# DeltaNet and mixture of depths: 16x16 block inverses on VectorE, joined on TensorE, without the way over DRAM

## The chip, the cores and the metric

One NeuronCore of a Trainium2 chip runs the program. The metric is the device time of one execution in microseconds (us). A profiled execution has a span, from its first to its last instruction, and a time of its own, a little longer.

## The reference

The program has two parts. The first is a delta-rule recurrence over 768 tokens for 4 batches and 8 heads, with 48 values per head:

```python
for t in range(S):
    kt, vt, bt = (k_n[:, :, t], v[:, :, t], beta[:, :, t, None])
    y[:, :, t] = np.einsum('bhd,bhde->bhe', q[:, :, t], state)
    v_old = np.einsum('bhde,bhd->bhe', state, kt)
    state = state + bt[:, :, :, None] * np.einsum('bhd,bhe->bhde', kt, vt - v_old)
```

Here `k_n` is k divided by its norm. The second part takes y as x (768 tokens of 384 values per batch), scores every token with `w_gate`, chooses 128 tokens of each batch, and gives those `x + sigmoid(score) * relu(x @ w1) @ w2`. All other tokens pass through. All arithmetic is in float32.

## The kernel before, in words

**Chunks.** The recurrence runs over chunks of 64 tokens. A chunk works on 2 batches and 8 heads at once, 16 (batch, head) pairs; there are 24 chunks, 12 for each half of the batches. Inside a chunk the recurrence is a triangular system of 64 unknowns. Its matrix comes from the products of all keys of the chunk with each other (`products`, tile `g`). It is solved by inverting the two 32x32 triangles on its diagonal, and then using them and the 32x32 block below: `z` (L667) makes M from the lower block and the lower inverse, and the recurrence makes W = T V and adds M W1.

**Elimination.** Four chunks are inverted together (`eliminate(e)`, L513, six of them): 4 partition groups of 32 (batch and half) hold 32 triangles each, and VectorE works on all 128 partitions with up to 32x32 values in each. To bring one triangle into one partition's row, the first elimination uses a VectorE transpose (L523). The others write `g` to DRAM (`spill`, L464) and read it back turned, into tile `a` (L528). After scaling (L563), 27 steps follow, each with a product (`mul`, L586, into `tmp`), a row (L572) and an addition (`add`, L592); the last six rows are done one by one. A product with a table of factors ends it (L597). The first and last elimination turn their result back with VectorE (L600), the last then copies it to tile `tt` by DMA; the four others write it to DRAM (`ad`, L604) and read it back turned into `tt` (L610).

**Recurrence.** Chunk i (`recur`, L711) is a chain between TensorE and ScalarE: `mm_r` (L734, keys times state), copy to `v` (L741), `mm_w` (L749 with `tt`, or L755 in four 32-row parts with `g`), copy W1 to `wsb` (L771), `mm_m` (L766), two copies to `wbd` (L775), `mm_s` (L783, the new state in `psta`), copy to `s` (L788). Beside it `mm_q` (L797) and `mm_p` (L809) make the output, `out_x` copies it (L815), and VectorE scores it (L829). Transposes of k and q (L395), their products (L454) and the ranking of tokens (`ranking`, L881) are put in between. The dense part (`depths`, L977, with L1025 and L1041) comes mostly after the last chunk.

**Order.** A planner in the kernel (`Plan`, L25) decides the order of every engine's operations when the program is built. Each operation has an engine, a duration, operations it depends on, a latency to its users, a priority, and buffers that it takes and gives back. The planner plays this through in time and writes out the order in which operations start. Where it sees TensorE idle, it puts in matmuls of ones as fillers (L301). Its durations do not wait for anything on the chip; they only set the order. All instructions are written out one after the other, without loops on the chip. PSUM has one tile for the state and a ring of three pairs of banks (`pair`) for all else.

Of the kernel before, what the change touches and what calls it, by code (L numbers as in the profile page):

```python
# [15 lines left out]
P = 128  # L16
# [141 lines left out]
def kernel(  # L158
# [30 lines left out]
    assert NB == HC and NCH % BC == 0 and H == 8  # L189
    DP = 64  # L190
# [36 lines left out]
    ring("a", 2, [HC, HC])  # L227
    rings["gd"] = [dram.tile([P, NB, C], FP32, name=f"gd{m}") for m in range(3)]
    plan.ring("gd", 3)
    ad = [dram.tile([P, HC, HC], FP32, name=f"ad{m}") for m in range(2)]  # L230
    ring("mb", 1, [HC, HC])
    ring("zt", 3, [GP, HC])
    ring("tt", 2, [NB, C])
# [19 lines left out]
    def maker(eng, own=0.0, lat=0.15):  # L253
# [9 lines left out]
        ("PE", 0.0, 0.22), ("ACT", 0.0, 0.12), ("DVE", 0.12, 0.2), ("POOL",), ("SP",))]  # L263
# [25 lines left out]
    wsb = sbuf("wsb", [GP, D])  # L289
# [21 lines left out]
    ds = [slice(x * DP, x * DP + D) for x in range(2)]  # L311
    four = [(0, 0), (1, 1), (0, 1), (1, 0)]
# [4 lines left out]
    def constants():  # L317
# [6 lines left out]
        for t in rings["tt"]:  # L324
            nc.gpsimd.memset(t, 0.0)
# [87 lines left out]
    def prep(i):  # L413
# [72 lines left out]
        for nm in "kq":  # L486
# [4 lines left out]
            n["t" + nm] = pe(0.48, emit, n["l" + nm] + late, v, take=[kx, (nm + "t", i)],  # L491
                             give=[("q", i)] if nm == "q" else [], work=512,
                             lat=0.22 if first else LATE["turn"], **h)
            if first and nm == "k":
                n["ek"] = [on(0.38, put(par, eng), [n["tk"]], v, give=[kx], **h)
                           for par, on, eng in ((0, act, nc.scalar), (1, dve, nc.vector))]
            else:
                n["e" + nm] = [act(0.6, both, [n["t" + nm]], v, give=[kx], **h)]
        gt = [kb] + [("g", e)] * (i % BC == 0)
        if first:  # L500
            n["g"] = pe(1.0, first_products, n["ek"], u, take=gt, work=1024, hard=True)
            n["eg"] = [act(0.59, out_g, [n["g"]], u, give=[kb], hard=True)]
        else:
            n["g"] = pe(0.75, products("kt", kb), [*n["ek"], N[e * BC].get("g")], u, take=gt,
                        work=1024, lat=LATE["g"])
            n["eg"] = [act(0.6, out_g, [n["g"]], u, give=[kb])]
            n["sg"] = sp(0.6, spill, n["eg"], u, take=[("gd", e)] * (i % BC == 0), lat=4.6)
        v = 10 * i - 14
        n["w"] = pe(0.75, products("qt", kw), n["eq"] + n["ek"] + [N.get(("end", 0))], v,
                    work=1024, take=[kw, ("p", i)], lat=LATE["p"])  # L510
        n["ep"] = [dve(0.7, out_p, [n["w"]], v - 200, give=[kw])]

    def eliminate(e):  # L513
        u = 40 * e - 50
        s = N["e", e] = {}
        first = e == 0

        over = 0 < e < NE - 1
        hard = dict(hard=first)

        def turn_in():
            if first:
                nc.vector.transpose(out=got("a", e),  # L523
                                    in_=got("g", e)[:, :, HC:].rearrange("p n t -> p t n"))
                return
            for par in range(2):
                for hf, rows in ((0, lo[par]), (1, hi[par])):
                    nc.sync.dma_start(  # L528
                        out=got("a", e)[rows],
# [3 lines left out]
        def diag():  # L533
            nc.vector.tensor_scalar_max(
                nrm[:, 0], got("a", e).rearrange("p i c -> p (i c)")[:, ::HC + 1], 1e-30)
# [15 lines left out]

        def table():

            b, sign = bh[e % 2], -1 if over else 1
            nc.gpsimd.affine_select(  # L555
                out=got("mb", e), pattern=[[sign, HC], [-sign, HC]], base=0,
                in_=(b[:, :, None] if over else b[:, None, :]).to_broadcast([P, HC, HC]),
                channel_multiplier=0, compare_op=ALU.is_ge, fill=0.0)

        def scale():  # L560
            a = got("a", e)
            b = bh[e % 2]
            nc.vector.tensor_tensor(out=a, in0=a, op=ALU.mult,  # L563
                                    in1=(b[:, None, :] if over else b[:, :, None])
                                    .to_broadcast([P, HC, HC]))
            nc.vector.memset(a.rearrange("p i c -> p (i c)")[:, ::HC + 1], 1.0)

        def row(i, j):
            a = got("a", e)
            to, of = (a[:, :j, i], a[:, :j, j]) if over else (a[:, i, :j], a[:, j, :j])  # L570
            by = a[:, j, i:i + 1] if over else a[:, i, j:j + 1]
            nc.vector.scalar_tensor_tensor(out=to, in0=of, scalar=by, in1=to,  # L572
                                           op0=ALU.mult, op1=ALU.add)

        def step(j):
            w = HC - 2 - j

            def view():
                return tmp[j % 2][:, :w * j].rearrange("p (i c) -> p i c", c=w if over else j)

            def mul():
                a = got("a", e)
                x = ((a[:, j:j + 1, j + 2:], a[:, :j, j:j + 1]) if over else
                     (a[:, j + 2:, j:j + 1], a[:, j:j + 1, :j]))
                shape = [P, j, w] if over else [P, w, j]
                nc.vector.tensor_tensor(out=view(), op=ALU.mult, in0=x[0].to_broadcast(shape),  # L586
                                        in1=x[1].to_broadcast(shape))

            def add():
                a = got("a", e)  # L590
                to = a[:, :j, j + 2:] if over else a[:, j + 2:, :j]
                nc.vector.tensor_tensor(out=to, in0=to, in1=view(), op=ALU.add)  # L592
            return mul, add, 0.075 + 1.04e-3 * w * j

        def final():
            a = got("a", e)
            nc.vector.tensor_tensor(out=a, in0=a, in1=got("mb", e), op=ALU.mult)  # L597

        def turn_out():
            nc.vector.transpose(out=got("g", e)[:, :, HC:].rearrange("p n t -> p t n"),  # L600
                                in_=got("a", e))

        def out_a():
            nc.sync.dma_start(out=ad[e % 2], in_=got("a", e))  # L604


        def back(par):
            def emit():
                for hf, rows in ((0, lo[par]), (1, hi[par])):
                    nc.sync.dma_start(out=got("tt", e)[rows, :, hf * HC:(hf + 1) * HC],  # L610
                                  in_=ad[e % 2][rows].rearrange("n i c -> i n c") if over else
                                  got("g", e)[rows, :, HC:])
            return emit
# [10 lines left out]
        N["nrm", e] = s["nt"] = dve(0.2, turn_n, [s["sc"]], u + 2)  # L624
        s["mb"] = pool(1.6, table, [s["sc"]], u, take=[("mb", e)])
        last = dve(1.45, scale, [s["sc"]], u, **hard)

        nxt, rest = last, [last]
        for j in range(1, HC - 1):
            if j >= HC - 4:  # L630
                rows = [dve(0.16, (lambda i=i, j=j: row(i, j)), [nxt, *rest], u, **hard)
                        for i in range(j + 1, HC)]
                nxt, rest = rows[0], rows
                continue
            mul, add, dur = step(j)
            m = dve(dur, mul, [nxt], u, **hard)
            nxt = dve(0.13 + 1.04e-3 * j, (lambda j=j: row(j + 1, j)), [nxt, *rest], u, **hard)
            rest = [dve(dur, add, [m, *rest], u, **hard)]
            if j == HC - 8:
                N["late", e] = rest[0]  # L640
        N["end", e] = last = dve(1.22, final, [nxt, *rest, s["mb"]], u, give=[("mb", e)], **hard)
        if over:
            x = plan.add("DVE", 0.0, lambda: None, [last], u, lat=1.5)
            s["to"] = sp(0.69, out_a, [x], u, take=[("tt", e)], give=[("a", e)], lat=4.0)
# [492 lines left out]
```

## Time and profile before

| | |
|---|---|
| median of 4 runs | 344.81 us (340.48 to 348.99) |
| the profiled execution's own time | 338.85 us |
| its span | 337.1 us |
| granted TensorE clock, mean | 0.852 |
| instructions | 17,651 |
| TensorE matmuls, weight loads | 7866, 7866 |
| DMA | 37.60 MB, mean 112 GB/s |

In the lines of the profile, PE is TensorE's matmuls, PEld its weight loads, DVE VectorE, ACT ScalarE, POOL GpSimd, SP the engine that issues most DMAs. `out<-in` names tiles, `128x64` is partitions by elements, `64*64` the rows and columns of TensorE's array that an instruction uses, `x32` a number of instructions. A float32 matmul of the kernel is two matmul instructions with a weight load each; transposes and bfloat16 ones are one. In the chain of waits, each piece of the span is put down to the instruction, DMA or queue that the end of the program waited for; "issue" is time in which an engine waited for nothing that the profile shows. In the list of DMA queues, the columns are packets, MB and the share of 16 engines' time; the kind "instruction" brings the engines' code. A row of the windows has the stretch, its length, then busy time (and number of instructions) of PE, PEld, DVE, ACT and POOL, then the granted clock, the DMA engines' busy share and GB/s.

### The profile page before, as it was taken

To read this page: it belongs to the slowest core of one execution; us is meant where nothing else is said; L and a number is where in the kernel's file an instruction comes from. 1 tells how busy PE (TensorE), PEld (TensorE's weight loads), DVE (VectorE), ACT (ScalarE), POOL (GpSimd) and SP (SyncE) were. 2 spreads that over 40 slices of the span, in tenths; PEclk is the share of its full clock that TensorE was granted. 3 is DMA by queue.
4 is the path that set the end of the run, shared out by engine and by line. 5 is a ranking of instruction groups with operands and counts; after the bars stand their busy time and mean duration, and the time that the engine had idled before them with its cause. 6 is when DMAs were issued, how large, how long until landed. Compare 5 with 4: busy or idle time off the path is not lost.

```text
span 337.1 us, 17651 instructions
## 1 busy us (share of the span) xinstructions
PE 280.9 (83%) x7866; PEld 221.9 (66%) x7866; DVE 217.8 (65%) x856; ACT 131.6 (39%) x299; POOL 26.8 (8%) x51
## 2 busy tenths in 40 slices
PE   7498496997959876976977979989988999999994
PEld 4446445776737765864866868878777788576571
DVE  4169999499993999679585499798455423522000
ACT  2219203554513545342552554443646344112110
POOL 8120002001000100010000010000020000031011
PEclk9769878799876978795696795696988799999999
DMA  6796687362688667576987756343631021110000
GB/s 95 133 159 137 152 216 130 70 162 46 160 204 187 147 167 164 117 150 145 200 219 192 141 107 124 72 94 64 126 75 51 4 47 31 26 49 25 25 23 23
DMA packets 127691, 37.60 MB, mean 112 GB/s; under 512 B 119552, under 2 KB 123776, under 8 KB 127616
## 3 DMA queue, kind: packets, MB, share of 16 engines
q1 hardware_dynamic: 120048, 33.65, 46.7%
q10 hardware_dynamic: 7056, 1.26, 2.3%
q0 software_dynamic: 512, 1.57, 1.5%
q8 instruction: 61, 1.00, 1.3%
q14 instruction: 14, 0.11, 0.1%
HBM read 23.10 MB, written 12.85 MB: 107 GB/s over the span
## 4 chain that ended last, share of the span: by engine, by line
PE 48%; DMA 16%; DVE 16%; issue 8%; SPq 6%; ACT 5%; POOLq 0%; ACTq 0%; DVEq 0%
PE pair L1025 5%; DMA ad<-a 5%; PE psta L783 5%; PE pair L1041 5%; PE pair L809 5%; PE pair L766 4%; DVE tmp L586 4%; DMA tt<-ad 4%; PE pair L301 4%; DVE a L592 4%; PE pair L797 3%; PE psta L734 3%; SPq L610 3%; PE pair L749 3%; PE pair L454 3%
## 5 line engine op out<-in xcount | busy, mean ns | idle before, releaser
L586 DVE TENSOR_TENSOR tmp<-a 128x29 f32<-128x29 f32 (+8 forms) x162 | 54.4, 336 | 0.0
L592 DVE TENSOR_TENSOR a<-a,tmp 128x29 f32<-128x29 f32 (+8 forms) x162 | 53.1, 328 | 0.0
L572 DVE SCALAR_TENSOR_TENSOR a<-a 128x28 f32<-128x28 f32 (+29 forms) x198 | 46.0, 240 | 0.1
L704 DVE TENSOR_TENSOR psta<-v,nnT 128x192 f32<-128x192 f32 x44 | 16.0, 365 | 27.1 <-ACT v L741 26.4
L783 PE MATMUL psta<-wbd,k 128*64 128x96 f32 x352 | 27.3, 307 | 4.7 <-ACT wbd L775 4.5
L775 ACT COPY wbd<-pair 64x384 f32<-64x384 f32 x48 | 22.7, 473 | 19.2 <-PE pair L766 17.8
L809 PE MATMUL pair<-wbd,p 128*64 128x96 f32 x384 | 27.8, 303 | 0.0
L766 PE MATMUL pair<-wsb,zt 32*32 32x48 f32 x768 | 23.0, 212 | 5.7 <-ACT wsb L771 4.8
L301 PE MATMUL pair<-warm 128*128 128x512 bf16 x84 | 27.6, 470 | 0.0
L783 PEld LDWEIGHTS psta<-wbd,k 128*64 128x64 f32 x352 | 21.4, 174 | 8.8 <-ACT wbd L775 7.5
L766 PEld LDWEIGHTS pair<-wsb,zt 32*32 32x32 f32 x768 | 19.4, 112 | 10.0 <-ACT wsb L771 8.7
L1025 PE MATMUL pair<-xeT,w_sb 128*64 128x128 f32 x384 | 23.5, 275 | 2.2 <-ACT hT L1032 2.2
L555 POOL TENSOR_SCALAR_AFFINE_SELECT mb<-bh 128x1024 f32<-128x1024 f32 x6 | 10.5, 1752 | 175.3 <-DVE bh L547 114.3
L809 PEld LDWEIGHTS pair<-wbd,p 128*64 128x64 f32 x384 | 22.8, 176 | 1.6
L1025 PEld LDWEIGHTS pair<-xeT,w_sb 128*64 128x64 f32 x384 | 20.9, 137 | 4.0 <-ACT hT L1032 2.9
L917 DVE TENSOR_SCALAR_CACHE_REDUCE mk<-rep 128x64 bf16<-128x64 f32 (+10 forms) x22 | 13.3, 607 | 15.7 <-ACT rep L910 15.6
L1041 PE MATMUL pair<-w_sb,hT 128*64 128x384 f32 x128 | 22.3, 490 | 0.0
L797 PE MATMUL pair<-s,qt 64*64 64x48 f32 x704 | 20.1, 262 | 2.2 <-issue 2.2
L771 ACT COPY wsb<-pair 128x384 f32<-128x384 f32 x24 | 11.5, 479 | 24.7 <-PE pair L749 21.3
L797 PEld LDWEIGHTS pair<-s,qt 64*64 64x64 f32 x704 | 17.0, 174 | 5.7 <-issue 4.3
L741 ACT COPY v<-psta 128x384 f32<-128x384 f32 x22 | 10.6, 480 | 23.8 <-PE psta L734 22.5
L460 ACT COPY g<-pair 128x512 f32<-128x512 f32 x24 | 14.0, 593 | 13.8 <-PE pair L444 7.5
(113 smaller groups left out, 454.8 us busy)
## 6 DMA issues: line engine op xcount, KB each, us to landing
gd<-g SPq DMA_DIRECT2D x20, 256.0 KB
q<-in_q_dram SPq DMA_DIRECT2D x48, 96.0 KB
v<-in_v_dram SPq DMA_DIRECT2D x48, 96.0 KB
out_dram<-x SPq DMA_DIRECT2D x20, 192.0 KB
k<-in_k_dram SPq DMA_DIRECT2D x36, 96.0 KB
a<-gd SPq DMA_DIRECT2D x20, 128.0 KB
ad<-a SPq DMA_DIRECT2D x4, 512.0 KB
tt<-ad SPq DMA_DIRECT2D x16, 128.0 KB
```

Source lines behind the costliest of these rows:

```text
L301: nc.tensor.matmul(rings[name][k][:, 0], lhsT=warm[:, :P], rhs=warm, start=True, stop=True)
L572: nc.vector.scalar_tensor_tensor(out=to, in0=of, scalar=by, in1=to, op0=ALU.mult, op1=ALU.add)
L586: nc.vector.tensor_tensor(out=view(), op=ALU.mult, in0=x[0].to_broadcast(shape), in1=x[1].to_broadcast(shape))
L592: nc.vector.tensor_tensor(out=to, in0=to, in1=view(), op=ALU.add)
L704: nc.vector.tensor_tensor(out=to[:, b], in0=x, in1=y, op=ALU.mult)
L766: nc.tensor.matmul(pw[hi[par], bb, y], lhsT=zt[lo[par], bb * GI + y], rhs=wsb[lo[par], bb * GI + y], start=False, stop=True, skip_group_ch ...
L775: nc.scalar.copy(wb[half[par], :, par].rearrange("p (b r) d -> p b r d", b=2), heads(kw)[half[par]])
L783: nc.tensor.matmul(psta[half[a % 2], r // 2, r % 2 * 2 * D:(r % 2 + 1) * 2 * D], lhsT=t[:, a], rhs=wb[:, a].rearrange("p h d -> p (h d)"), ...
L797: nc.tensor.matmul(py[half[bb], rt, x * D:(x + 1) * D], lhsT=qt[half[rt], bb * 2 + h4, half[par]], rhs=s_old[half[rt], bb * 2 + h4, par], ...
L809: nc.tensor.matmul(py[half[bb], rt, h4 * 2 * D:(h4 + 1) * 2 * D], lhsT=t[:, a], rhs=wb[:, a].rearrange("p h d -> p (h d)"), start=(c == 0 ...
L1025: nc.tensor.matmul(ps[half[x]], lhsT=w1_sb[:, t, c0:c0 + C], rhs=got("xeT", b)[:, t], start=(t == 0), stop=(t == KD - 1))
L1041: nc.tensor.matmul(got("pair", b, "o")[c0:c1, 0, :DM], lhsT=got("hT", b)[:, f, c0:c1], rhs=w2_sb[:, f], start=(f == 0), stop=(f == KF - 1))
```

## The change

Each 32x32 triangle is taken as two 16x16 triangles and the block below. VectorE inverts the 64 small triangles of each partition, two at a time in each instruction: 14 steps of a product and an addition, each dependent on the one before. The single rows are gone. Two VectorE transposes then bring the result into tiles `ta` and `tb`, in all eliminations alike; `ad`, `tt` and their DMAs are gone. The way from `g` over DRAM into `a` stays.

For each chunk TensorE joins the halves: `up_z` is 32 products of 32x32 with 16 columns (64 instructions), ScalarE copies them to `zs`, `up_t` puts the transposed triangle in PSUM through the identity (4 products) and adds 32 more products, 72 instructions in all, and ScalarE copies the result back to `ta`. `z` then uses `ta`. `mm_w` has the 32 products of the L755 form for all chunks. `mm_m` uses four 32x32 tiles of TensorE's array where it used two, so M lies on all 128 partitions (`zt` at half the width), and W1 is copied there in three pieces. GpSimd makes the factor table in two 16x16 parts. The planner's durations are set anew. In the built order TensorE has 11,690 matmuls; 36 fillers remain of 84.

```diff
+    QC = HC // 2
-    ad = [dram.tile([P, HC, HC], FP32, name=f"ad{m}") for m in range(2)]
-    ring("zt", 3, [GP, HC])
-    ring("tt", 2, [NB, C])
+    ring("zs", 2, [GP, QC])
+    ring("zt", 3, [GI, HC])
+    ring("ta", 2, [NB, HC])
+    ring("tb", 2, [NB, HC])
...
         def step(j):
-            w = HC - 2 - j
+            w = QC - 1 - j
...
+            def mul():
+                a, shape = blocks("a"), [P, 2, w, j]
+                nc.vector.tensor_tensor(
+                    out=view(), in0=a[:, :, j + 1:, j:j + 1].to_broadcast(shape),
+                    in1=a[:, :, j:j + 1, :j].to_broadcast(shape), op=ALU.mult)
+
+            def add():
+                a = blocks("a")[:, :, j + 1:, :j]
+                nc.vector.tensor_tensor(out=a, in0=a, in1=view(), op=ALU.add)
...
+        def turn_a():
+            nc.vector.transpose(out=got("ta", e).rearrange("p n t -> p t n"), in_=whole("a"))
+
+        def turn_b():
+            nc.vector.transpose(out=got("tb", e).rearrange("p n t -> p t n"),
+                                in_=whole("a").rearrange("p i c -> p c i"))
...
+        four_rows = [(rows[bb], hf) for bb in range(GB) for hf, rows in ((0, lo), (1, hi))]
...
+        def up_z():
+            g, t, ps = got("g", e), got("ta", e), bank(0)
+            for x in range(GP):
+                for rows, hf in four_rows:
+                    c0 = HC if e == 0 else hf * HC
+                    nc.tensor.matmul(ps[rows, x], lhsT=g[rows, n0 + x, c0:c0 + HC],
+                                     rhs=t[rows, n0 + x, QC:], start=True, stop=True)
+
+        def out_z():
+            nc.scalar.copy(got("zs", i), bank(0))
+
+        def up_t():
+            ta, tb, z, ps = got("ta", e), got("tb", e), got("zs", i), bank(1)
+            for rows, _ in four_rows:
+                nc.tensor.matmul(ps[rows], lhsT=ident[rows, rows], rhs=ta[rows, n0:n0 + GP, QC:],
+                                 start=True, stop=False, skip_group_check=True)
+            for x in range(GP):
+                for rows, _ in four_rows:
+                    nc.tensor.matmul(ps[rows.start:rows.start + QC, x],
+                                     lhsT=tb[rows, n0 + x, :QC], rhs=z[rows, x],
+                                     start=False, stop=True, skip_group_check=True)
+
+        def out_t():
+            nc.scalar.copy(got("ta", e)[:, n0:n0 + GP, QC:], bank(1))
...
         def mm_w():
-                    if not n["direct"]:
-                        nc.tensor.matmul(pw[half[par], bb, y],
-                                         lhsT=got("tt", e)[half[bb], ch * GP + a],
-                                         rhs=x[half[bb], a], start=(y == 0), stop=False,
-                                         skip_group_check=True)
-                        continue
                     for rows in (lo, hi):
-                        nc.tensor.matmul(pw[rows[par], bb, y],
-                                         lhsT=got("g", e)[rows[bb], ch * GP + a, HC:],
+                        nc.tensor.matmul(pw[rows[par], bb, y], lhsT=t[rows[bb], ch * GP + a],
...
         def mm_m():
-                for bb in range(GB):
-                    for par in range(2):
-                        nc.tensor.matmul(pw[hi[par], bb, y], lhsT=zt[lo[par], bb * GI + y],
-                                         rhs=wsb[lo[par], bb * GI + y], start=False,
-                                         stop=True, skip_group_check=True)
+                for bb, par in four:
+                    rows = at[bb][par]
+                    nc.tensor.matmul(pw[hi[par], bb, y], lhsT=zt[rows, y], rhs=w1[rows, y],
+                                     start=False, stop=True, skip_group_check=True)
...
         def out_w1():
-            nc.scalar.copy(wsb.rearrange("p (b r) d -> p b r d", b=2), heads(kw))
+            pw = heads(kw)
+            nc.scalar.copy(w1[:3 * HC], pw[:3 * HC, 0])
+            for par in range(2):
+                nc.scalar.copy(w1[hi[par]], pw[lo[par], 1])
```

## The prediction

> **What bounds the kernel now.** I read the page first, then the chain of waits, then TensorE's timeline, then the DMA packets. The page (parts 1, 3 and 4):
>
> ```profile
> PE 280.9 (83%) x7866; PEld 221.9 (66%) x7866; DVE 217.8 (65%) x856; ACT 131.6 (39%) x299; POOL 26.8 (8%) x51
> q8 instruction: 61, 1.00, 1.3%
> PE 48%; DMA 16%; DVE 16%; issue 8%; SPq 6%; ACT 5%; POOLq 0%; ACTq 0%; DVEq 0%
> ```
>
> No engine is full. The chain is PE for half, and DMA, DVE and SPq for 38%. Where DVE and DMA stand on it, the chain from 82 to 100 us shows the way from the end of an elimination to the first product that uses it:
>
> ```profile
> 87.65 0.10 DVE a L592
> 87.75 4.19 DMA ad<-a
> 92.37 1.53 SPq L610
> 94.55 2.77 DMA tt<-ad
> 97.36 0.99 PE pair L673 x62
> ```
>
> 9.6 us pass between 87.75 and 97.36. The same stretch takes 11.6 us from 119.01, 8.9 from 151.63 and 9.3 from 187.86: 39.4 us in all. This is what the change goes for. But 8% of the chain, some 26 us, is "issue": PE waits for nothing that is computed. TensorE's timeline around 53 and 171 us shows where:
>
> ```profile
> 51.80 1.17 PE L673 MATMUL pair<-g 32*32 32x32 f32 x96
> 52.83 0.76 PE L755 MATMUL pair<-v,g 32*32 32x48 f32 x60
> 55.87 0.27 PE L755 MATMUL pair<-v,g 32*32 32x48 f32 x4 [2.29 <-issue]
> ...
> 169.85 0.50 PE L797 MATMUL pair<-s,qt 64*64 64x48 f32 x20
> 171.36 0.43 PE L797 MATMUL pair<-s,qt 64*64 64x48 f32 x12 [1.01 <-issue]
> ```
>
> PE stops in the middle of one operation, 60 instructions into 64, whose operands have long been there. Queue q8 tells why. It brought 1.00 MB in 61 packets, 16 KB each; PE's program has 15,820 instructions (7866 matmuls, 7866 weight loads, 88 others), so a packet holds 256 of them, 128 pairs of load and matmul. I listed the packets' times and numbered PE's instructions in program order. If packet n brings the instructions from number 464 + 256n on, no packet's first matmul starts earlier than 1.34 us after the packet has ended, in any of the 61, and 17 start within 1.8 us: there PE was waiting for its own code. The packet at 53.51 to 54.43 is the one that PE resumes with at 55.87. Nor is a packet begun early: where PE stood at such a border, the next one began 0.8 to 2.8 us after it went on. So the code comes in a loop with one packet under way: start, 0.9 to 1.5 us of packet, 1.4 us until PE goes on, then the next. Five borders at which PE waited follow one at which it had waited too; from one to the next took 3.82, 4.33, 4.04 us (around 172 us, DMA share 0.82) and 3.98, 3.73 us (240 to 248 us, share near 0.45). Never in the trace do two packets start less than 3.46 us apart. The rate of matmuls agrees (windows of 10 us):
>
> ```profile
> 255.00:265.00 10.00, 8.64 (x316) 7.51 (x310) 4.80 (x23) 6.22 (x15) 0.00 (x0) 0.83 0.17 43
> 265.00:275.00 10.00, 8.66 (x343) 7.58 (x341) 4.74 (x17) 4.47 (x10) 0.00 (x0) 1.00 0.01 3
> 275.00:285.00 10.00, 10.00 (x307) 8.73 (x299) 3.13 (x14) 4.79 (x12) 0.00 (x0) 1.00 0.27 64
> ```
>
> 31 to 34 matmuls per us is 128 in 3.7 to 4.2 us: in its densest stretches the kernel already runs close to the pace of that loop.
>
> **The change part by part.**
>
> *Elimination on VectorE.* Out go 27 steps of three instructions and six single rows. In come 14 steps of two, on 2wj elements (w = 15 - j), 1120 in one pass. Rows of L586 go from 199 ns at 56 elements to 388 at 225: 137 ns + 1.1 ns each. So 28 x 0.137 + 2 x 1.23 = 6.3 us, and 0.04 between dependent ones (L542 to L547 show it): 7.3. The first elimination scales from 22.88 us on (L563 halved, 0.7; small ones 0.2), runs its steps (7.3), lets the same v products through (1.2), multiplies by the table (L597, 1.2) and transposes once (1.95): ready at 35.4 us, where now the first z product starts at 51.8. The second transpose (1.95) lies beside TensorE's first products.
>
> *No turn over DRAM.* The 39.4 us above go, with 24 DMA issues of SP (0.3 to 1.7 us each in the L610 rows). Late next on this path would be up_z, ACT, up_t, ACT, z: about 4 us at full clock.
>
> *TensorE, time.* Per chunk up_z adds 64 instructions and up_t 72. The nearest row is z, 32x32 in four tiles: 32 start within 263 ns, 383 until the next operation (168.15). So 0.65 and, with the four copies by the identity, 0.85. The W product has 64 instructions everywhere (0.73, L755 at 63.95) instead of 32 (0.50 to 0.61): +0.2 in 19 chunks. M W1 in four tiles instead of two goes from 0.80 (L766) to about 0.4. Together +1.3 us a chunk, 31 us in all, of which idle PE and 48 dropped fillers can take most.
>
> *TensorE, code.* 136 pairs x 24 + 32 x 19 - 48 fillers = 3824 pairs more: 11,690 instead of 7866, and 23,456 instructions, 91.6 packets instead of 61.8. In the built order the first up_z stands at packet 4.4 and the last product of the recurrence at 85.8: 81.4 packets. Now the same stretch (4.4 to 56.05, 35.7 to 288.6 us) has 51.6, at 4.9 us each with all waits.
>
> *ScalarE.* Two more copies per chunk (L910, 270 ns), and three pieces of W1 instead of one copy of 479: 0 to 0.5 us on each step of the recurrence, at most 12 us. Taken at nothing, as the wait for code covers it; if that cover is gone it is in the rival below. GpSimd's smaller tables, the loads that SP can now issue earlier and the new prices of the plan are taken at nothing too: none of them ends a wait on the chain, and what the prices move is in the order I counted.
>
> *The sum.* PE comes to up_z at 36 us: DVE is ready at 35.4, and the products ordered before it end at 36 now. From there code is the bound. For the pace I take the pair at the DMA share nearest to what remains (3.98 and 3.73, mean 3.86), since the DRAM turn is gone and the same loads are spread over a longer time. 36 + 81.4 x 3.86 = 350. After the last product of the recurrence come 48.6 us as now (288.6 to 337.1; the same products, slow ones, four packets only), and 1.75 us lie around the span (338.85 - 337.1): 401 us, 62 more than this execution's 338.85. The median of the runs is 344.81, 6 above it; with the same distance 406.
>
> The Trainium skill speaks against this reading. "Runtime: NRT & Kernel Launch", section "Instruction fetch mechanics", says that code is fetched in 16 KiB blocks while the current one executes, at a cost that is mostly hidden. The block size agrees with the 61 packets of 16 KB here; the hiding does not, with 17 borders at which PE stood. By that rule the sum would be the first rival's; by the rows it is 401.
>
> **The rivals.**
>
> *Code doesn't bind, the kernel gets faster.* Its place is the same loop: with the DRAM turn gone the packets might come quicker. It decides at 3.11 us per packet (36 + 81.4 x 3.11 + 50.35 = 339.5). Smallest parts of separate packets (0.8 to begin, 0.9, 1.35) make 3.05; against it stands the 3.46 that no pair undercuts, the window with DMA share 0.01 included. Then the sum is 338.85 - 16 (first elimination) - 39 (DRAM) - 10 (M W1) + 31 + 4 x 4 (the new way after each of four eliminations) = 321 if PE's new work lies all on the path, and 290 if none of it does: 305.
>
> *Code just keeps pace, no change.* 3.1 to 3.2 us per packet, 340 to 346 by the same sum. It needs a pace that no stretch shows.
>
> *Code and waits add up.* A packet holds only 128 pairs, fetched one ahead. Where those include a wait for ScalarE, or run at half clock (the z blocks take 413 instead of 263 ns where the granted clock is 0.5), the loop starts late and loses again. The densest part now, 205 to 288 us, has 4.46 us per packet with such waits: 36 + 363 + 50 = 449, 455 against the median. For it: PE will stand more, and the clock may fall. Against it: a chunk's waits spread over 3.4 packets instead of 2.1.
>
> **How the numbers follow.** Forecast 0.66 (3.6 to 4.2 us per packet: 380 to 428 on this execution's basis, 386 to 434 on the median's); code and waits together 0.21; no change 0.04; faster 0.09. The low end, 368, is the smallest spacing seen, 3.46; the high end, 455, is 4.46. That leaves out the faster case, no change and a little at the top. A difference of 2% is about what measuring can tell from none. Faster by over 2%: 0.09; within: 0.04; slower: 0.87.
>
> **What would show it.** Queue q8 with 91 packets, most borders within 1.8 us of their packet's end, and 28 to 34 matmuls per us through the whole recurrence. "Issue" grows from 8% to a leading share of the chain; PE's holes lie in the middle of operations. The first z products no longer wait for DVE at 51.8, and yet the first W product (packet 10.0) comes at about 36 + 5.6 x 3.86 = 57.6 us, later than the 52.8 of now. DVE's busy time falls from 218 to about 115 us (some 29 us of each elimination become 12), and no DMA ad or tt remains. The steps of the recurrence (from one W1 copy to the next) take 12 to 14 us instead of 9.9. I am wrong if the packets follow at 3 us or less: then the first W product comes near 42 us and the steps take 8 to 9 us.

## The result, and the profile after

The changed kernel takes 417.86 us (median of 10 runs, 416.08 to 420.77); the kernel before took 342.85 us beside it (15 runs, 334.53 to 348.99). The ratio is 1.2455, with a 95% interval of 1.2386 to 1.2523. Executions of one kernel can be fast or slow; the medians take in both and the ratios the fast ones alone, so a ratio is not the quotient of the medians (1.219 here). The profiled execution took 419.42 us, its span 417.7 us, at a mean granted clock of 0.740 (before 0.852).

The page of the changed kernel, parts 1, 3 and 4:

```profile
PE 331.7 (79%) x11690; PEld 275.0 (66%) x11690; DVE 160.8 (39%) x512; ACT 153.6 (37%) x395; POOL 22.4 (5%) x56
q8 instruction: 91, 1.49, 1.5%
PE 69%; issue 16%; ACT 8%; DVE 3%; DMA 2%; ACTq 1%; POOLq 0%
```

VectorE and the DMA are nearly off the path: DVE falls from 16% of the chain to 3%, DMA and SPq from 22% to 2%. What the change was written for has happened. But the span is 80.6 us longer, and the chain is now TensorE (69%) and "issue" (16%, 67 us). Queue q8 has the 91 packets that were counted ahead.

TensorE's timeline from the first joining product on (start, length in us, line, operation; in brackets the idle time before it) shows what that "issue" is:

```profile
35.97 0.88 PE L652 MATMUL pair<-ta,g 32*32 32x16 f32 x70
39.66 0.98 PE L652 MATMUL pair<-ta,g 32*32 32x16 f32 x58 [2.81 <-issue]
40.44 0.66 PE L662 MATMUL pair<-ta,ident 32*32 32x128 f32 x8
40.84 0.75 PE L666 MATMUL pair<-zs,tb 32*16 32x16 f32 x62
43.66 0.18 PE L666 MATMUL pair<-zs,tb 32*16 32x16 f32 x1 [2.07 <-issue]
```

58 + 8 + 62 = 128 matmuls run in 1.9 us; then TensorE stands for 2.07 us, two instructions before the end of an operation of 64, with no wait for data that the profile shows. 128 pairs are one packet of q8, and a packet of q8 lies in this stop: it ran from 41.24 to 42.25. `up_z` begins at 35.97, 15.8 us earlier than the first `z` used to, and the code behind it comes slowly.

By windows (stretch, length, busy time and number of instructions of PE, PEld, DVE, ACT and POOL, then clock, DMA share and GB/s), the whole recurrence runs at nearly one pace; four of its stretches:

```profile
36.00:80.00 44.00, 30.19 (x1302) 26.37 (x1303) 18.49 (x62) 14.48 (x40) 2.38 (x4) 0.61 0.56 128
160.00:200.00 40.00, 31.41 (x1314) 27.48 (x1320) 9.18 (x22) 15.11 (x41) 0.00 (x0) 0.79 0.46 98
240.00:280.00 40.00, 33.47 (x1290) 29.39 (x1280) 24.37 (x82) 15.78 (x44) 1.42 (x2) 0.63 0.22 44
280.00:320.00 40.00, 33.41 (x1176) 29.69 (x1164) 12.85 (x51) 16.68 (x46) 2.08 (x2) 0.54 0.26 58
```

29 to 33 matmuls per us, whether the DMA share is 0.56 or 0.22 and whether VectorE works 9 us of 40 or 24. So neither the DMA's load nor VectorE's sets the pace. The clock goes from 0.54 to 0.79 over these stretches, and the pace does not follow it in order.

The groups that belong to the change (busy time, mean ns of one; idle time before them and its releaser):

```profile
L652 PE MATMUL pair<-ta,g 32*32 32x16 f32 x1536 | 23.7, 198 | 9.3 <-issue 7.6
L666 PE MATMUL pair<-zs,tb 32*16 32x16 f32 x1536 | 20.2, 184 | 13.3 <-issue 13.2
L766 PE MATMUL pair<-w,zt 32*32 32x48 f32 x768 | 18.0, 235 | 11.5 <-ACT w L774 7.3
```

The joining products are cheap to execute, 44 us in all. They are not cheap to bring: 3072 of them and 192 copies by the identity are 25.5 packets.

I listed q8's packets and TensorE's borders (instruction 464 + 256n) as in the prediction, for every kernel below. A border is the place in TensorE's program where the instructions of one packet end and those of the next begin. It counts as waited for when its first matmul starts within 1.8 us of the packet's end; the time is that from the border before to this one. Only borders inside the recurrence are in this table, after the first joining product or, where nothing is joined, after the first `z`:

```
kernel         borders  waited for   mean us, waited   mean us, others   mean us, all
before            50        14            3.78              5.09             4.72
after             82        44            3.70              4.58             4.11
b_code            75        37            3.70              4.76             4.24
b_time            51        13            3.80              4.96             4.67
a_few             60        28            3.78              4.70             4.27
a_few_time        61        17            3.71              4.58             4.34
a_code           107        78            3.80              4.52             4.00
a_fill            83        21            3.44              4.50             4.23
a_two             82        45            3.91              4.62             4.23
h1_turn           55        18            3.67              4.75             4.40
h2_turn_four      55        25            3.79              4.56             4.21
h3_turn_wide      49         6            3.60              4.96             4.80
h4_wide_four      49        11            3.61              5.03             4.71
```

Counted over every packet, the changed kernel has 47 of 91 borders that were waited for. The others took longer in the mean, with their packet landed earlier. I read the table so: a packet takes the longer of two things, its fetch, about 3.7 us, or its own work and waits (for ScalarE, in wide products, at half clock). The first is shown by the borders; which work or wait made each of the others long I did not separate.

### The profile page after: what moved, and what is told of

The parts are those of the page before. It is cut to its first block, busy times and chain, and to the rows that moved or that the text cites. A ratio compares the mean times of both kernels' runs of the same rounds, so it can differ in the third digit from the quotient of the medians.

```text
span 417.7 us, 25025 instructions
## 1 busy us (share of the span) xinstructions
PE 331.7 (79%) x11690; PEld 275.0 (66%) x11690; DVE 160.8 (39%) x512; ACT 153.6 (37%) x395; POOL 22.4 (5%) x56
## 4 chain that ended last, share of the span: by engine, by line
PE 69%; issue 16%; ACT 8%; DVE 3%; DMA 2%; ACTq 1%; POOLq 0%
PE pair L812 7%; PE psta L786 7%; PE pair L458 7%; PE pair L800 5%; PE pair L652 5%; PE pair L756 5%; PE pair L1027 4%; PE pair L1043 4%; PE psta L741 4%; PE pair L766 4%; PE pair L666 3%; PE pair L399 3%; ACT wbd L778 3%; PE pair L681 3%; PE pair L662 2%
## 5 line engine op out<-in xcount | busy, mean ns | idle before, releaser
L652 PE MATMUL pair<-ta,g 32*32 32x16 f32 x1536 | 23.7, 198 | 9.3 <-issue 7.6
L666 PE MATMUL pair<-zs,tb 32*16 32x16 f32 x1536 | 20.2, 184 | 13.3 <-issue 13.2
L666 PEld LDWEIGHTS pair<-zs,tb 32*16 32x16 f32 x1536 | 20.2, 100 | 15.2 <-issue 14.4
L652 PEld LDWEIGHTS pair<-ta,g 32*32 32x32 f32 x1536 | 20.8, 131 | 12.2 <-issue 8.9
L471 DVE TENSOR_TENSOR p<-pair,up 128x512 f32<-128x512 f32 x24 | 16.4, 685 | 28.8 <-PE pair L458 28.7
L766 PE MATMUL pair<-w,zt 32*32 32x48 f32 x768 | 18.0, 235 | 11.5 <-ACT w L774 7.3
L756 PE MATMUL pair<-v,ta 32*32 32x48 f32 x1536 | 22.3, 234 | 5.5 <-issue 3.6
L756 PEld LDWEIGHTS pair<-v,ta 32*32 32x32 f32 x1536 | 18.2, 118 | 7.8 <-issue 4.0
L681 PE MATMUL pair<-ta,g 32*32 32x32 f32 x768 | 16.7, 230 | 7.7 <-issue 4.0
L597 DVE TENSOR_TENSOR a<-a,tmp 128x28 f32<-128x28 f32 (+6 forms) x84 | 21.0, 251 | 2.4
```

Of the source, the lines that this page charges most:

```text
L652: nc.tensor.matmul(ps[rows, x], lhsT=g[rows, n0 + x, c0:c0 + HC], rhs=t[rows, n0 + x, QC:], start=True, stop=True)
L666: nc.tensor.matmul(ps[rows.start:rows.start + QC, x], lhsT=tb[rows, n0 + x, :QC], rhs=z[rows, x], start=False, stop=True, skip_group_check ...
L681: nc.tensor.matmul(ps[at[bb][par], y], lhsT=g[hi[bb], a, :HC], rhs=t[hi[bb], a], start=True, stop=True)
L756: nc.tensor.matmul(pw[rows[par], bb, y], lhsT=t[rows[bb], ch * GP + a], rhs=x[rows[bb], a], start=(y == 0), stop=False, skip_group_check=True)
L766: nc.tensor.matmul(pw[hi[par], bb, y], lhsT=zt[rows, y], rhs=w1[rows, y], start=False, stop=True, skip_group_check=True)
```

## The experiments

Theory (code): TensorE's program comes one packet of 256 instructions at a time, and every packet costs some 4 us. First rival (TensorE's time): the new products themselves, at a lower clock, make the time. Second rival (waits): the chain over ScalarE and VectorE sets the end, and the code runs beside it. In the first five runs what is added or taken out stands inside one operation, whose duration in the planner is left as it was, so the order of operations stays that of the kernel they start from.

**b_code: the kernel before, with more code and no more data.** Ahead of each chunk's `z`:

```diff
+            for m in range(136):
+                r = hi[m % 2]
+                nc.tensor.matmul(got(*key)[r, 0, 511:512], lhsT=warm[r, :HC], rhs=warm[r, :1],
+                                 start=True, stop=True)
```

> The kernel before, with 136 pairs of weight load and matmul added to every chunk, as many as the change adds for the join, but tiny ones: 32x32 bfloat16 ones with a single column, into a part of PSUM that nobody reads. They stand ahead of the z products. PE's program grows from 61.8 to 87.3 packets of code. If the supply of code is what slowed the change: 77 packets in the stretch from 36 us to the end of the recurrence, at the 4.04 us per packet of the changed kernel, are 312 us; with 36 before and 50 after, 398 us. If it was TensorE's time: at the 8.5 ns per instruction of the z blocks 136 are 1.2 us a chunk, 28 us in all if none is hidden, so at most 371 us.

423.71 us in one run, beside 344.33 of the kernel before on the same chip: 79 us more, as much as the whole loss of the change (75 us), with the eliminations, the DRAM turn and M W1 as they were. The page, and the row of the added pairs:

```profile
PE 340.6 (81%) x11130; PEld 278.8 (66%) x11130; DVE 217.8 (52%) x856; ACT 132.0 (31%) x299; POOL 26.8 (6%) x51
q8 instruction: 87, 1.43, 1.5%
PE 59%; issue 15%; DVE 15%; DMA 5%; ACT 4%; SPq 0%; ACTq 0%; POOLq 0%; DVEq 0%
L670 PE MATMUL pair<-warm 32*32 32x1 bf16 x3264 | 49.3, 160 | 23.2 <-issue 22.9 <-DVE csum L942 0.3
```

DMA and SPq fall from 22% of the chain to 5% although the DRAM turn is still in the program: it now lies beside the wait for code. The clock fell too, from 0.839 in the kernel before on that chip to 0.757: the added pairs are enough for that, it needs none of the change's products. The pairs are busy for 49.3 us themselves, so this run alone does not part code from TensorE's time; the next one does.

**b_time: the kernel before, with more of TensorE's time and little code.** In the same place:

```diff
+            for _ in range(7):
+                nc.tensor.matmul(got(*key)[:, 0], lhsT=warm[:, :P], rhs=warm, start=True, stop=True)
```

> The kernel before, with 7 of its fillers (512 columns of ones, some 0.22 us each at full clock) added to every chunk ahead of the z products: 1.5 us of TensorE's time per chunk, as much as the two new steps of the join take, but only 7 instead of 136 pairs of code (63.1 packets instead of 61.8). If code is the cause: 1.3 packets are 5 us, and the fillers' time lies partly beside waits that are there anyway: 345 to 365 us. If TensorE's time is the cause of the slowdown, this kernel must lose as much as the change does or more, over 400 us; all of its 37 us in a row would make 380.

340.55 us in one run, against 344.33: nothing lost that shows beside the 334.53 to 348.99 over which the kernel before spreads. The group of the added matmuls and the page's q8:

```profile
L669 PE MATMUL pair<-warm 128*128 128x512 bf16 x168 | 42.7, 396 | 1.0 <-DVE p L467 0.8 <-DVE csum L940 0.3
```

```profile
q8 instruction: 63, 1.03, 1.3%
```

The added matmuls take about what all the joining products of the changed kernel take (44 us), and nearly what b_code's pairs take (49.3), in 1.3 packets instead of 25.5. TensorE's time alone falls as the cause. Not all of the 42.7 us went into time in which TensorE had stood: its busy time is 292.5 us, against 280.9 in the profile of the kernel before, and its clock 0.945. A higher clock may have paid for a part, so this run does not rule out the low clock as a helper; that rests on the borders, where TensorE stands until its packet has come.

**a_few: the changed kernel, each join step in four wide products**, with one triangle's block for all eight, so it leaves out the right joins of the seven others: 70.6 packets instead of 91.6. The first step, and the second likewise:

```diff
-            for x in range(GP):
-                for rows, hf in four_rows:
-                    c0 = HC if e == 0 else hf * HC
-                    nc.tensor.matmul(ps[rows, x], lhsT=g[rows, n0 + x, c0:c0 + HC],
-                                     rhs=t[rows, n0 + x, QC:], start=True, stop=True)
+            for rows, hf in four_rows:
+                c0 = HC if e == 0 else hf * HC
+                nc.tensor.matmul(ps[rows], lhsT=g[rows, n0, c0:c0 + HC],
+                                 rhs=t[rows, n0:n0 + GP, QC:], start=True, stop=True)
```

> The changed kernel, with each of the join's two steps done by 4 wide products (128 columns, the first triangle's weights for all eight) in place of 32 narrow ones; the copies and all waits stay. It leaves out the right joins of seven triangles in eight. 2688 pairs and 21 packets of code fewer (70.6 instead of 91.6). If code is the cause: 60.4 packets at 4.04 us, with 36 before and 50 after, 330 us, at most 345 as other waits begin to show. If TensorE's time is the cause: about 0.95 us less per chunk at full clock, 1.4 at half: 23 to 34 us off 418, 384 to 395 us.

343.63 us in one run, against 344.33. Taking 21 packets of code out takes 74 us out of the changed kernel: 3.5 us a packet. The time of the join steps' products falls by less, from 43.9 us to 24.4 (rows of 11.7 and 12.7).

**a_few_time: a_few with six matmuls of ones per chunk.**

```diff
+            for _ in range(6):
+                nc.tensor.matmul(got(*kj)[:, 0], lhsT=warm[:, :P], rhs=warm, start=True, stop=True)
```

> As the kernel with 4 wide products per step, and the time of TensorE that this saves is given back by 6 fillers of 512 columns per chunk (1.3 us) ahead of up_z: 71.7 packets of code. If code is the cause: 5 us for 1.1 packets and some of the fillers' 31 us: 335 to 365 us. If TensorE's time is the cause: as the changed kernel, about 418 us.

352.56 us in one run, 8.9 us over a_few, for 36.8 us of added matmuls in its group's row (L650). The kernel is far from the 418 us that TensorE's time would make. How much of the added time counts, one run of each can't tell: 8.9 us is less than the spread of the kernel before.

**a_code: the changed kernel with b_code's pairs on top.**

```diff
+            for m in range(136):
+                r = slice(m % 4 * HC, (m % 4 + 1) * HC)
+                nc.tensor.matmul(got(*kz)[r, 1, 511:512], lhsT=warm[r, :HC], rhs=warm[r, :1],
+                                 start=True, stop=True)
```

> The changed kernel with 136 one-column pairs of 32x32 in bf16 more in each chunk, ahead of its z products: 3264 pairs, 25.5 packets, no data waited for. Code theory: the recurrence holds 81.4 + 25.5 = 106.9 packets, and at the pace of the changed kernel, 4.04 us, the run takes 36 + 106.9 x 4.04 + 52 = 520 us (505 to 545). TensorE's time theory: the added pairs cost at most their own execution, 3264 x about 9 ns = 29 us, so 418 to 447 us.

514.04 us in one run. The group of the added pairs, and the page's q8 and chain:

```profile
L679 PE MATMUL pair<-warm 32*32 32x1 bf16 x3264 | 34.5, 165 | 41.2 <-issue 38.2 <-ACT wbd L782 2.1 <-ACT rep L916 0.4
```

```profile
q8 instruction: 117, 1.92, 1.6%
PE 66%; issue 25%; ACT 5%; DMA 2%; DVE 1%; ACTq 1%; POOLq 0%
```

34.5 us of matmuls cost 96 us of time, 3.77 us for each of the 25.5 packets: the same dose of code cost 79 us in b_code. It is the plainest of the runs, since 78 of 107 borders were waited for, against 44 of 82 without the pairs.

The Trainium skill, in "Runtime: NRT & Kernel Launch", section "Instruction fetch mechanics", has the fetch mostly hidden behind the block that executes. Its block of 16 KiB agrees with q8's packets; the hiding does not hold for a program of small matmuls, where 128 pairs execute in 1.9 us and the next block took 3.7 us.

**a_fill: the changed kernel with a_few_time's six matmuls per chunk**, to see what the half clock costs.

> The changed kernel with six more matmuls of ones (512 columns, 0.2 to 0.5 us each) in each chunk ahead of its first joining product: 288 instructions more, 92.7 packets. It asks what the half clock costs in the changed kernel. Code theory, clock without effect: 1.1 packets more, the fillers run while PE would wait: 416 to 424 us. Code theory, and the half clock made some packets longer than their fetch: the granted clock rises from 0.74 to 0.85 or more and the pace from 4.04 to about 3.86 us per packet: 36 + 82.5 x 3.86 + 52 = 406, 400 to 412. TensorE's time theory: 144 x 0.3 = 43 us more, 440 to 465.

435.6 us (4 runs), ratio to the kernel before 1.2951 (1.2837 to 1.3066), and the clock rose from 0.740 to 0.831. The time lies between what the theories expected: 17.7 us more than the changed kernel, for the 42.7 us that the row of the added matmuls (L650, 120 of the 144 are in the trace) holds. The table shows what they did: only 21 of 83 borders are still waited for, those take 3.44 us instead of 3.70, and yet the mean of all goes from 4.11 to 4.23. Read by the model above, work put into a packet fills the wait at its end, and what is over makes the packet longer. A higher clock did not pay for itself here, but what the low clock costs by itself this run can't tell, since the added work hides it.

**a_two: the changed kernel with M W1 in two tiles again**, M laid out for that, and W1 copied once.

```diff
-                for bb, par in four:
-                    rows = at[bb][par]
-                    nc.tensor.matmul(pw[hi[par], bb, y], lhsT=zt[rows, y], rhs=w1[rows, y],
-                                     start=False, stop=True, skip_group_check=True)
+                for bb in range(GB):
+                    for par in range(2):
+                        nc.tensor.matmul(pw[hi[par], bb, y], lhsT=zt[lo[par], bb * GI + y],
+                                         rhs=wsb[lo[par], bb * GI + y], start=False,
+                                         stop=True, skip_group_check=True)
```

> The changed kernel with M W1 in two tiles again and W1 copied once, all else of the change kept; as many instructions of TensorE, 91 packets. Code theory: the four tiles were worth next to nothing in the changed kernel, since its code is as long: 415 to 424 us, ratio to the kernel before 1.21 to 1.25. Rival, TensorE's time and the chain through W1: 24 x 0.4 = 10 us longer than the changed kernel, 428 or more.

426.59 us (4 runs), ratio 1.2658 (1.2539 to 1.2777) against the changed kernel's 1.2455 (1.2386 to 1.2523). The median lies between what the two expected (415 to 424, and 428 or more), the ratio above the code theory's 1.21 to 1.25. So the four tiles are worth 9 us by the medians, some 7 by the ratios, even in a kernel that waits for code; the rival, with 24 x 0.4 us, was nearer. The row of M W1, in a_two:

```profile
L766 PE MATMUL pair<-wsb,zt 32*32 32x48 f32 x768 | 29.8, 242 | 6.9 <-issue 4.4 <-ACT wsb L772 2.4
```

In the changed kernel it has 18.0 us and 11.5 of idle time: 11.8 us less of TensorE's time for 4.6 more of waiting. Of the 24 packets that hold most of an M W1, 12 end at a border that was waited for, in each of the two profiles. These took 4.02 us in a_two and 3.85 in the changed kernel, the 12 others 5.07 and 4.53. So M W1's time counts mostly where code is not waited for. That is not the whole of the difference between the two profiles: 32 waited borders without M W1 took 3.82 us in a_two and 3.64 in the changed kernel, and why is not known.

**h1_turn: the kernel before without the DRAM turn, nothing else of the change.** VectorE transposes each whole inverse in place, all chunks use the 64-instruction form of the W product:

```diff
-        over = 0 < e < NE - 1
+        over = False
...
-            s["to"] = dve(1.95, turn_out, [last], u, take=[] if first else [("tt", e)],
-                          give=[("a", e)], **hard)
-        if not first:
-            x = sp(1.38, back(0), [s["to"]], u, lat=5.0)
-            s["bk"] = [x, sp(1.38, back(1), [s["to"], x], u, lat=5.0)]
+            s["to"] = dve(1.95, turn_out, [last], u, give=[("a", e)], **hard)
```

> The kernel before with one part of the change alone: no table is turned over DRAM, VectorE transposes each whole 32x32 inverse. Its eliminations stay 27 steps, and nothing is joined by TensorE; the W product has 64 instructions in all chunks (608 pairs, 4.75 packets more than before). Code theory: the first z product starts at 52 as before, then 51.65 + 4.75 = 56.4 packets at 4.04 us make 228, the tail 50: 330 us, 4 per cent less than before (322 to 340), since the 39 us of waits go and 19 us of code come. Rival, that waits and not code set the end: 343 - 39 + 10 = 314 or less. If VectorE's eliminations are the next bound, 335 to 345.

341.58 us (10 runs) beside 340.91; ratio 1.011 (1.0027 to 1.0193). A miss: I expected 4 per cent less; the time lies in the 335 to 345 that I gave for VectorE's eliminations as the next bound. The page of h1_turn:

```profile
q8 instruction: 66, 1.08, 1.3%
PE 60%; DVE 18%; issue 10%; ACT 7%; DMA 2%; ACTq 1%; SPq 1%; POOLq 0%; DVEq 0%
```

Nearly all of the turn is off the chain (DMA and SPq were 22% of it and are 3%), and the time is what it was: PE went from 48% to 60%, VectorE, "issue" and ScalarE took 2% more each. The recurrence has 4.75 packets more, which at the 3.7 us of a waited packet are 18 us; and the packets that are not waited for take 4.75 us each.

**h2_turn_four: h1_turn with M W1 in four tiles** (the lines of a_two the other way round).

> The same as h1_turn, and M W1 in four tiles as in the changed kernel, with W1 copied in three pieces. The number of instructions of TensorE stays the same. Code theory: where code is the bound the shorter M W1 gains little, 0 to 5 us below h1_turn. Rival, TensorE's time and the chain of waits: 24 x 0.4 = 10 us below h1_turn. ScalarE's three pieces instead of one copy could cost 0 to 12 us.

332.67 us (4 runs), ratio 0.9821 (0.9607 to 1.0035): 9 us less than h1_turn, the rival's number, though the two intervals (h1_turn's begins at 1.0027) just overlap.

**h3_turn_wide: h1_turn with the wide table kept**, so that the W product has 32 instructions everywhere and 5.7 packets go. VectorE transposes into `tt`; ScalarE and VectorE move its lower halves, GpSimd clears them:

```diff
-            nc.vector.transpose(out=got("g", e)[:, :, HC:].rearrange("p n t -> p t n"),
+            nc.vector.transpose(out=got("tt", e)[:, :, :HC].rearrange("p n t -> p t n"),
...
+        def move(x, eng):
+            def emit():
+                t = got("tt", e)[hi[x]]
+                if eng is nc.scalar:
+                    eng.copy(t[:, :, HC:], t[:, :, :HC])
+                else:
+                    eng.tensor_copy(t[:, :, HC:], t[:, :, :HC])
+            return emit
```

> The kernel before without the turn over DRAM, but with the wide table kept: VectorE transposes into it, ScalarE and VectorE move its lower halves, GpSimd clears them. The W product keeps 32 instructions everywhere, so there are about 60.8 packets, 5.7 fewer than in h1_turn. Code theory: 52 + about 50.7 x 4.04 + 50 = 307 if code alone were the bound, 10 to 23 us below h1_turn unless VectorE's eliminations or the new copies (about 3 us per elimination, 15 in all) end the waits first: 310 to 330. Rival, waits alone: the same as h1_turn, or up to 15 us longer for the copies.

332.48 us (5 runs), ratio 0.9803 (0.9693 to 0.9914): 9 us less than h1_turn, just short of the 10 to 23 expected, and not down to the 307 that code alone would allow. Its profiled execution took 339.18 us, 2% over its median. Only 6 of 49 borders are waited for there, so code can set little of its end, and the rest is left to the chain of waits and TensorE's time.

**h4_wide_four: h3_turn_wide with M W1 in four tiles.**

> h3_turn_wide with M W1 in four tiles as in the changed kernel; 61 packets, as many instructions of TensorE as h3_turn_wide. In h3_turn_wide only few packets are waited for, so here the chain of waits and TensorE's time count: 24 x 0.4 = 10 us less, 320 to 326 us, a ratio of 0.94 to 0.96 to the kernel before. Rival, that code sets the end here too (52 + 51 x 4.04 + 50 = 308 is its floor): the gain would be under 4 us, 328 to 333.

332.08 us (6 runs), ratio 0.9858 (0.9767 to 0.9948): no gain over h3_turn_wide, where I expected 10 us; the number is the one of the rival, but not its reason, since 11 of 49 borders are waited for. The groups give another reason. In h3_turn_wide, then in h4_wide_four:

```profile
L779 PE MATMUL pair<-wsb,zt 32*32 32x48 f32 x768 | 25.2, 222 | 2.1 <-ACT wsb L784 1.9
L779 PE MATMUL pair<-w,zt 32*32 32x48 f32 x768 | 14.1, 210 | 16.7 <-ACT w L786 15.2
```

and, from the full list of groups of h4_wide_four, the copies of W1:

```profile
L786 ACT COPY w<-pair 32x192 f32<-32x192 f32 x48 | 14.8, 309 | 1.3
L784 ACT COPY w<-pair 96x192 f32<-96x192 f32 x24 | 7.6, 315 | 17.1 <-PE pair L762 16.8
```

Three pieces one after the other are 0.315 + 2 x 0.309 = 0.93 us, where the one copy of h3_turn_wide takes 0.479. M W1 itself falls by 11.1 us, from 25.2 to 14.1, and TensorE's idle time before it grows by 14.6, from 2.1 to 16.7, of which 15.2 are waits for the last copy of W1. So what the four tiles save goes into the wait for the copies that they need. The same rows of h1_turn and h2_turn_four:

```profile
L759 PE MATMUL pair<-wsb,zt 32*32 32x48 f32 x768 | 25.5, 217 | 9.4 <-ACT wsb L764 4.6 <-issue 4.6
L759 PE MATMUL pair<-w,zt 32*32 32x48 f32 x768 | 15.5, 218 | 11.7 <-ACT w L766 8.2 <-issue 3.3
```

There M W1 falls by 10.0 us and the idle time before it grows by 2.3 alone, as it grew by 4.6 from a_two to the changed kernel. In both, TensorE already stood 7 to 9 us before M W1 with the two tiles, about half of it or more in "issue", where h3_turn_wide stood 2.1. This fits the reading that the longer copies end while TensorE stands for code; that they do is not shown copy by copy.

## Why the prediction was right, and where its numbers were off

The forecast was 406 us, the time is 417.86, in the range and by the mechanism forecast: code. b_code and a_code add code alone and lose 79 and 96 us; a_few takes it out and gains 74; b_time adds time alone and loses nothing.

**The sum, term by term.** `up_z` starts at 36.0 us, as predicted. The last product of the recurrence ends at 369.4, and 48.3 us follow (predicted 48.6). So 81.4 packets took 333.4 us, 4.10 each, where the sum had 3.86. That is the term of the sum that was mis-sized: 81.4 x 0.24 = 19 us, and with it the sum gives the 419.4 us of the profiled execution, where it had 401. The forecast came closer than that by luck: it added 6 us because the profiled execution of the kernel before lay 6 below its median, and that of the changed kernel lies 1.6 above. The step that was off is the choice of the pace: I took the mean of two pairs of borders that were both waited for, as if all would be. Such borders did take 3.70 us here; but 38 of 82 were not waited for and took 4.58. The rival that code and waits add up, with 4.46, was right for these, though not for all: 4.10 lies between the two. How much of the 4.58 is the low clock and how much waits and wide products stays open after a_fill. The forecast of 386 to 434, at 3.6 to 4.2 us per packet, holds both the time and the pace.

**The first W product** came at packet 10.0 as counted, at 59.6 us instead of 57.6 (before 52.8). From W1 copy to W1 copy the steps take 13.1 us in the mean (12 to 14 predicted, 9.9 before), single ones 7.2 to 25.9. Matmuls per us: 29 to 34 over the whole recurrence (28 to 34).

**"Most borders"** within 1.8 us: 47 of 91, barely so. **"Issue"** doubled to 16% of the chain, but PE leads with 69%, so that sign did not come as forecast. As I read it, TensorE still executes the last packet while code is on its way (mean clock 0.54 to 0.85 in the windows of the recurrence), and the profile gives that time to PE.

**VectorE** is busy for 160.8 us, not about 115. The first elimination was ready at 34.5 us (35.4 predicted). It also began earlier, at 21.48 instead of 22.88; from there it took 13.0 us where the sum had 12.6, so the steps were priced nearly rightly. What was wrong is the 29 us an elimination that they replace. 29 is the sum of the rows, and in the kernel before these lie over one another: all its DVE rows together make 275.7 us, its busy time 217.8. The rows' sum fell by 97 us, to 178.8, about as predicted; the busy time, which counts an overlap once, by 57. The rows now:

```profile
L597 DVE TENSOR_TENSOR a<-a,tmp 128x28 f32<-128x28 f32 (+6 forms) x84 | 21.0, 251 | 2.4
L591 DVE TENSOR_TENSOR tmp<-a 128x28 f32<-128x28 f32 (+6 forms) x84 | 20.3, 241 | 2.3
```

None of this touched the time, with VectorE at 3% of the chain.

**ScalarE**, taken at nothing: the pieces of W1 are 0.93 us instead of 0.48 in the changed kernel too, and two copies of 0.27 came per chunk. Beside M W1 in four tiles that cost less than the tiles gained (a_two is 9 us longer, not shorter). In h4_wide_four, where code is seldom waited for, it took back all that the tiles gave: the bound of 12 us was needed there.

**TensorE's prices** held where the clock was full: from `up_z` to the next operation 0.66 us (0.65), M W1 0.47 (0.4).

**The 39.4 us of the DRAM turn** were read from the chain of before as a gain that goes to whoever takes them away. h1_turn took them off the chain and gained nothing, h3_turn_wide, without the extra code, 2%. Right under that wait lay others. In h1_turn a part is code (18 waited borders); for h3_turn_wide, with TensorE 57%, VectorE 18% and ScalarE 7% of the chain, I have not separated them. That stays open.

Of the versions run, h3_turn_wide (0.9803, 0.9693 to 0.9914) and h4_wide_four (0.9858, 0.9767 to 0.9948) beat both kernels, by some 2% or less, with whole 32x32 inverses and the turn on VectorE; their intervals overlap.

## What to carry to other kernels

Count instructions as a resource of its own where TensorE's operations are small: here 256 of them cost about 3.7 us where TensorE waited for them, so a 32x32 float32 product of 16 columns, four instructions, costs 0.06 us of code where it executes in 0.02. Many products that take little time can make a kernel slower than few that take much. And before a wait is priced as a gain, look at what is next below it in the same stretch: removing 39 us of it was worth between nothing and 8 us here.

## What the runs showed of the hardware

- 16 KB of code, 256 instructions of TensorE, came with one packet under way, and in no kernel did two packets start less than 3.2 us apart in the recurrence; waited borders took 3.4 to 3.9 us in the mean of each kernel.
- 168 matmuls of 512 columns, 42.7 us of work, cost nothing that showed in b_time, whose clock was 0.945 where the kernel before had 0.839 on that chip. In the changed kernel six per chunk raised the clock from 0.740 to 0.831, and the time by 17.7 us.
- The granted clock fell with the packets: 0.877 in a_few (70.6), 0.740 in the changed kernel (91.6), 0.686 in a_code (117.1). The busy share of TensorE's matmuls fell as well, 81, 79 and 73%, but it does not order all the runs: b_code has 81% too, with a clock of 0.757. Why the clock fell is not shown.
